# Cosine attention and MLP mixer: early token weights, w2 placed in slot 1, k squares on GpSimd, a moved cast of v, three output tiles

## The chip, the cores and the metric

The kernel runs on one core of one Trainium2 chip. The metric is the device time of one execution in microseconds (us), as the median of several executions. The profile is one execution; its span, from first to last instruction, is 1.7 to 1.9 us shorter than the device time of the same execution.

## The reference

```python
def _attn_ref(q, k, v, tau):                  # q, k, v: (8, 12, 448, 64) float32, tau = 0.1
    q_n = q / (np.linalg.norm(q, axis=-1, keepdims=True) + 1e-06)
    k_n = k / (np.linalg.norm(k, axis=-1, keepdims=True) + 1e-06)
    scores = np.matmul(q_n, k_n.transpose(0, 1, 3, 2)) / tau
    ...                                       # softmax over the last axis
    return np.matmul(attn, v)

def _moe_ref(x, w_tok1, w_tok2, w_ch1, w_ch2):  # x: (8, 448, 768), heads side by side
    xt = x.transpose(0, 2, 1)
    h = np.maximum(xt @ w_tok1, 0.0) @ w_tok2     # 448 -> 256 -> 448, along the tokens
    u = x + h.transpose(0, 2, 1)
    h2 = np.maximum(u @ w_ch1, 0.0) @ w_ch2       # 768 -> 1536 -> 768, along the channels
    return u + h2
```

## The kernel before

The kernel works on pairs of heads; there are 48. Its main loop has slots: slot i computes the scores and exponentials of pair i, and beside them attention times v of the pair before, the token mixing of pairs still earlier, the normalisation of pairs to come, and pieces of the channel mixing of finished batches. A pair's q and k are squared and summed, turned into reciprocal norms on ScalarE, scaled on GpSimd (`kq`), transposed on TensorE (`pst`) and copied by VectorE (`qk`); only then can TensorE start its scores (`psS`). The parts concerned:

```python
outp = ctx.enter_context(tc.tile_pool(name="outp", bufs=2))      # output tiles ost
...
def weights_tok():                     # token weights, float32 in memory, cast by the DMA
    nc.gpsimd.dma_start(out=w1t[:, 0:NC, :], in_=moe_w_tok1[0:SM].rearrange(...))
    nc.gpsimd.dma_start(out=w1t[0:XR, NC, :], in_=moe_w_tok1[SM:S])
    w2n.append(mix.tile([P, TT, S], FP16, name="w2n", tag="gt16", bufs=1))
    nc.gpsimd.dma_start(out=w2n[0][:], in_=moe_w_tok2.rearrange(...))

def place_w2():                        # w2 in the token order of the other tiles
    nc.vector.tensor_copy(out=w2t[:, :, XR:S]..., in_=w2n[0][:, :, 0:SM]...)   # "main copy", 768 columns
    nc.vector.tensor_copy(out=w2t[:, :, S:S + XR], in_=w2n[0][:, :, SM:S])     # 128 columns

def place_w2_odd():
    nc.vector.tensor_copy(out=w2t[:, :, 0:XR], in_=w2n[0][:, :, SM:S])         # "last copy", 128 columns

def cast_v(n):                         # half n of v (six heads), float32 to float16
    (nc.vector if n < 3 else nc.gpsimd).tensor_copy(out=vts[n % NV]..., in_=vm[n]...)
...                                    # before the loop:
        squares_x(0, nc.scalar, nc.gpsimd)
        rnorms(0, 21, 33)
        scaled(1, nc.gpsimd)
...
        score_x(0)
        weights_tok()
        cast_vx(0)
        cast_v(0)
        scaled(2, nc.gpsimd)
        for i in range(NP_ALL + 2):
...                                    # slot i, first slots:
                score(i, 0, 2 if i < 4 else 0); score(i, 1); score(i, 2)
            for p in sum_at.get(i, ()):
                norm_sums(p)           # VectorE sums of squares
...
            casts()                    # slot 3: cast_v(1)
...
            if i: pv(i - 1)            # attention times v; VectorE: reciprocal, x
...
            if i in (0, 1, 2, 4): next_qk(i + 1)     # VectorE copies q and k of the next pair
...
            if i == 2: place_w2()      # end of slot 2
            if i == 3: place_w2_odd()  # end of slot 3
```

Of the kernel before, what the change touches and what calls it, by code (L numbers as in the profile page):

```python
# [22 lines left out]
def kernel(  # L23
# [12 lines left out]
    nc = tc.nc  # L36

    B, H, S, E = q.shape
# [5 lines left out]
    NC = 3  # L44
    SM = P * NC
# [22 lines left out]
    mix = ctx.enter_context(tc.tile_pool(name="mix", bufs=2))  # L68
    outp = ctx.enter_context(tc.tile_pool(name="outp", bufs=2))
    ps = ctx.enter_context(tc.tile_pool(name="ps", bufs=2, space=bass.MemoryType.PSUM))  # L70
# [68 lines left out]

    def weights_tok():  # L140
        nc.gpsimd.dma_start(out=w1t[:, 0:NC, :], in_=moe_w_tok1[0:SM].rearrange("(p c) t -> p c t", c=NC))
        nc.gpsimd.dma_start(out=w1t[0:XR, NC, :], in_=moe_w_tok1[SM:S])
        w2n.append(mix.tile([P, TT, S], FP16, name="w2n", tag="gt16", bufs=1))
        nc.gpsimd.dma_start(out=w2n[0][:], in_=moe_w_tok2.rearrange("(tt p) s -> p tt s", p=P))

    def place_w2():
        nc.vector.tensor_copy(out=w2t[:, :, XR:S].rearrange("t a (c p) -> t a c p", c=NC),
                              in_=w2n[0][:, :, 0:SM].rearrange("t a (p c) -> t a c p", c=NC))
        nc.vector.tensor_copy(out=w2t[:, :, S:S + XR], in_=w2n[0][:, :, SM:S])  # L149

    def place_w2_odd():
        nc.vector.tensor_copy(out=w2t[:, :, 0:XR], in_=w2n[0][:, :, SM:S])

# [33 lines left out]
    def squares_x(n, eq, ek):  # L187
        square(eq, sqx[0:XR, 0:6], xh(xq, n, 6))
        square(ek, sqx[:, 6:9], xh(xk, n, HP))
# [257 lines left out]
    def at(slots):  # L447
        got = {}
        for p, s in slots.items():
            got.setdefault(s, []).append(p)  # L450
        return got


    FIRST = NPAIR
    early_sq = {3: 0, 4: 1, 5: 1, 6: 3, 7: 4, 8: 5, 9: 5, 10: 6, 11: 7, 12: 8, 13: 9, 14: 9, 15: 10, 16: 11, 17: 11}
    sq_slot = {p: early_sq.get(p, p - 6) for p in range(3, NP_ALL)}
    sq_at = at(sq_slot)
    sum_at = at({p: s + 1 for p, s in sq_slot.items() if p < 8 or p >= 18})

    rn_at = {}  # L460
    for n in range(1, NHALF):
        for c0, c1 in ((0, 21), (21, 45)) if n < 4 else ((0, 45),):
            s = 1 + sq_slot[3 * n + (0 if c1 == 21 else 2)]
            rn_at.setdefault(s, []).append((n, c0, c1))
# [7 lines left out]
    xv_at = at({b: {1: 1, 2: 9}.get(b, 6 * b - 4) for b in range(1, B)})  # L472
    cast_at = at({n: {1: 3, 2: 6}.get(n, 3 * n - 2) for n in range(1, NHALF)})
    castx_at = at({n: {1: 2, 2: 6}.get(n, 3 * n - 2) for n in range(1, NHALF)})
# [37 lines left out]
    with tc.manual_schedule():  # L512
# [54 lines left out]
        tpose_main(0, pst, 1)  # L567
        squares_x(0, nc.scalar, nc.gpsimd)
        rnorms(0, 21, 33)
        scaled(1, nc.gpsimd)  # L570
# [17 lines left out]
        score_x(0)  # L588
        weights_tok()
        cast_vx(0)  # L590
        cast_v(0)
        scaled(2, nc.gpsimd)
        for i in range(NP_ALL + 2):
# [30 lines left out]
            def next_sq(ps):  # L624
                for p in ps:
                    norm_begin(p, nc.scalar if p < 18 else nc.gpsimd, nc.scalar if p == 3 else nc.vector if p in (10, 11, 12, 15) else nc.gpsimd)

# [20 lines left out]
            for p in sum_at.get(i, ()):  # L648
                norm_sums(p)
            if i < FIRST:  # L650
                norm_rn()
# [78 lines left out]
            if i == 2:  # L730
                place_w2()
            if i == 3:
                place_w2_odd()
        for p in ut_at.get(NP_ALL + 2, ()):
# [37 lines left out]
```

## Time and profile before

| | before |
|---|---|
| device time, median of the first three runs | 394.86 us (394.48 to 395.2) |
| span of the profile | 392.9 us |
| TensorE busy | 378.7 us, 96% |
| TensorE waiting for w2's copies, once | 1.14 us, at 27.5 us |
| TensorE waiting for an output tile, once | 1.13 us, at 94.8 us |
| VectorE without a hole | 30.7 to 35.0 us |

The lines behind this table stand in the prediction. In a timeline line the first number is the start in us from the beginning of the span, the second the length, then engine, source line, operation, output and input tiles with their shapes and the number of instructions merged into the line; the bracket at the end is the idle time just before it and what ended it. Starts also show more than lengths: the next instruction of an engine can start a little before the recorded end of the one before (in the prediction's lines VectorE's copy of 25.62 ends at 25.62 + 1.09 = 26.71, and the next starts at 26.63), so a cost on an engine's path is best read from start to start.

Four more lines of the kernel before carry the argument, two on VectorE, one on GpSimd, one on TensorE:

```profile
31.07 0.48 DVE L152 COPY w2t<-w2n 128x128 f16<-128x128 f16 x1
31.47 0.94 DVE L193 TENSOR_REDUCE ssq<-sq 128x12 f32<-128x768 f32 x1
30.67 0.82 POOL L211 TENSOR_TENSOR kq<-km,rn 128x384 f16<-128x384 f32 x1
51.57 0.35 PE L308 MATMUL psX<-qk 128*128 128x448 f16 x1 [0.51 <-ACT pt L302]
```

The first is w2's last copy, 0.3 us into the stretch of VectorE without a hole; the copy of pair 5's q and k, at 34.35, starts 3.28 us after it. The second is what VectorE does next, sums of squares, and the third is GpSimd's scaling of pair 5's k, which runs while the copy does. The fourth is a matmul of a later slot that waits 0.50 or 0.51 us for ScalarE in every kernel of this study; it serves as a milestone. What comes after it is 392.9 - 51.57 = 341.33 us.

### The profile page before, as it was taken

What the parts mean: (1) busy time and instruction counts of PE and PEld (TensorE: products, weight loads), DVE (VectorE), ACT (ScalarE), POOL (GpSimd) and SP (SyncE); (2) the same over time, 40 slices, a digit from 0 to 9 for tenths busy, and PEclk for the clock granted to TensorE, in tenths of its full rate; (3) what the DMA queues carried; (4) which work ended last, traced back from release to release, by engine and by line L of the source; (5) the groups of instructions that cost most, each with busy time, mean ns of one, the idle gap of its engine ahead of it and who ended that gap; (6) DMA issues with size and microseconds to landing.
All of it is one profiled execution on the core that took longest, in us unless ns stands there. A gap on an engine that the chain in (4) does not pass through costs nothing.

```text
span 392.9 us, 9076 instructions
## 1 busy us (share of the span) xinstructions
PE 378.7 (96%) x3658; PEld 228.5 (58%) x3658; DVE 193.5 (49%) x368; ACT 225.8 (57%) x411; POOL 209.6 (53%) x306
## 2 busy tenths in 40 slices
PE   8678999998999999999999999999999999999996
PEld 3346555665565656566556566566566566565554
DVE  5688758865344554545524645345534342333022
ACT  5998698843774639573676446673775536511400
POOL 4978486789267584868572947659561700000000
PEclk9899999999999999999999999999999999999999
DMA  7999999969968987999989899999982452013013
GB/s 203 276 238 253 246 236 215 227 138 264 209 131 190 202 183 179 222 183 208 205 199 198 175 245 216 166 189 182 242 142 56 123 123 68 16 57 102 5 40 120
DMA packets 137514, 67.51 MB, mean 172 GB/s; under 512 B 93248, under 2 KB 134016, under 8 KB 137472
## 3 DMA queue, kind: packets, MB, share of 16 engines
q1 hardware_dynamic: 133296, 61.36, 71.4%
q0 software_dynamic: 3632, 5.18, 7.4%
q8 instruction: 28, 0.46, 0.5%
q10 hardware_dynamic: 544, 0.39, 0.3%
q14 instruction: 14, 0.11, 0.1%
HBM read 43.38 MB, written 11.01 MB: 138 GB/s over the span
## 4 chain that ended last, share of the span: by engine, by line
PE 86%; ACT 6%; DVE 3%; DMA 2%; SPq 1%; issue 1%; ACTq 0%; DVEq 0%
PE psF L404 28%; PE psG L389 27%; PE psO L320 9%; PE psS L301 7%; PE psR L341 5%; PE psU L361 4%; ACT pt L302 3%; PE psO L322 3%; PE psX L308 2%; DMA out_dram<-ost 1%; DMA km<-in_k_dram 1%; PE psU L366 1%; PE pst L243 1%; ACT sq L178 1%; DVE ost L407 1%
## 5 line engine op out<-in xcount | busy, mean ns | idle before, releaser
L302 ACT ACTIVATE pt<-psS 128x896 f16<-128x896 f32 x141 | 119.0, 921 | 65.8 <-PE psS L301 65.5
L389 PE MATMUL psG<-ut,wc1t 128*128 128x448 f16 x576 | 119.5, 353 | 0.2
L404 PE MATMUL psF<-wc2t,gt 128*128 128x384 f16 (+2 forms) x684 | 117.3, 324 | 1.2 <-DVE ost L407 1.1
L391 ACT ACTIVATE gt<-psG 128x448 f16<-128x448 f32 x96 | 51.1, 557 | 73.2 <-PE psG L389 73.2
L404 PEld LDWEIGHTS <-gt 128*128 128x128 f16 x684 | 64.5, 98 | 48.4 <-issue 8.1
L389 PEld LDWEIGHTS <-wc1t 128*128 128x128 f16 x576 | 53.2, 98 | 52.5 <-issue 8.7
L211 POOL TENSOR_TENSOR kq<-km,rn 128x384 f16<-128x384 f32 x47 | 39.4, 837 | 80.9 <-ACT rn L204 80.7
L407 DVE TENSOR_TENSOR ost<-psF,ur 128x384 f32<-128x384 f32 (+2 forms) x57 | 31.4, 550 | 90.0 <-PE psF L404 86.6
L320 PEld LDWEIGHTS <-pt 128*128 128x128 f16 x1152 | 50.1, 97 | 8.4 <-issue 2.4
L320 PE MATMUL psO<-vt,pt 128*128 128x65 f16 x1152 | 52.4, 193 | 1.2 <-ACT pt L302 0.8
L326 DVE RECIPROCAL rec<-psO 128x8 f32<-128x8 f32 x48 | 9.9, 207 | 80.9 <-PE psO L322 80.9
L193 DVE TENSOR_REDUCE ssq<-sq 128x12 f32<-128x768 f32 (+1 forms) x49 | 45.1, 929 | 5.3 <-ACT sq L178 3.7
L322 PE MATMUL psO<-vx,pt 128*128 128x130 f16 x192 | 41.8, 218 | 0.0
L180 POOL TENSOR_TENSOR sq<-km 128x384 f32<-128x384 f32 x42 | 34.5, 823 | 13.2 <-DMA km<-in_k_dram 13.0
L211 POOL TENSOR_TENSOR kq<-qm,rn 128x384 f16<-128x384 f32 x47 | 39.5, 841 | 0.0
L301 PE MATMUL psS<-qk 64*128 64x448 f16 x282 | 36.1, 357 | 2.0 <-DVE qk L261 0.9
L327 DVE TENSOR_TENSOR x<-psO,rec 128x512 f16<-128x512 f32 x48 | 33.2, 691 | 1.7
L341 PE MATMUL psR<-x,w1t 128*128 128x128 f16 x384 | 29.2, 219 | 0.1
L309 ACT ACTIVATE pt<-psX 128x448 f16<-128x448 f32 x48 | 27.1, 564 | 3.3 <-PE psX L308 2.3
L361 PE MATMUL psU<-w2t,r 128*128 128x448 f16 x96 | 25.9, 353 | 1.5 <-DVE w2t L149 1.1
L180 POOL TENSOR_TENSOR sq<-qm 128x384 f32<-128x384 f32 x30 | 24.7, 822 | 2.4 <-DVE ssq L193 1.6
L341 PEld LDWEIGHTS <-w1t 128*128 128x128 f16 x384 | 23.8, 97 | 2.1 <-issue 0.3
(76 smaller groups left out, 320.8 us busy)
## 6 DMA issues: line engine op xcount, KB each, us to landing
vm<-in_v_dram SPq DMA_DIRECT2D x16, 576.0 KB, 5.0
out_dram<-ost SPq DMA_DIRECT2D x23, 384.0 KB, 3.1
qm<-in_q_dram SPq DMA_DIRECT2D x14, 576.0 KB, 5.1
km<-in_k_dram SPq DMA_DIRECT2D x14, 576.0 KB, 5.6
wc1t<-in_moe_w_ch_dram POOLq DMA_DIRECT2D x2, 1152.0 KB, 13.8
wc2t<-in_moe_w_ch_dram POOLq DMA_DIRECT2D x2, 1152.0 KB, 12.6
out_dram<-ost SPq DMA_DIRECT2D x9, 192.0 KB, 2.7
xq<-in_q_dram SPq DMA_DIRECT2D x7, 192.0 KB, 5.2
```

Of the source, the lines that this page charges most:

```text
L180: eng.tensor_tensor(out=out, in0=src, in1=src, op=ALU.mult)
L193: nc.vector.tensor_reduce(out=ssqs[p // HP % 3][:, lo + 6 * a0:lo + 6 * a1], in_=sq[p][:, a0:a1].rearrange("p a g e -> p (a g) e"), axis=A ...
L211: eng.tensor_tensor(out=kqs[n % 2][:, j, a, 0:NC, :].rearrange("p c (g e) -> p g c e", g=2), in0=src, in1=_bcast_free(rn, E), op=ALU.mult)
L301: nc.tensor.matmul(psS[:, g, 0:S], qk[r, P * c:P * (c + 1)], qk[r, 512:512 + S], start=True, stop=True)
L302: nc.scalar.activation(out=pt[:, 2 * S * c:2 * S * (c + 1)].rearrange("p (g s) -> p g s", g=2), in_=psS[:, :, 0:S], func=AF.Exp, scale=inv ...
L320: nc.tensor.matmul(psO[:, m, E1 * g:E1 * (g + 1)], pt[:, at:at + P], vt[:, 2 * j + g, c, 0:E1], start=(g == 0 and c == 0), stop=False)
L322: nc.tensor.matmul(psO[:, m, 0:2 * E1], pt[:, PX + P * m:PX + P * (m + 1)], vx[:, j, 0:2 * E1], start=False, stop=True)
L341: nc.tensor.matmul(psR[:, tt, :], w1t[:, m, tt * P:(tt + 1) * P], xs[p][:, m, :], start=(m == 0), stop=(m == NC))
L361: nc.tensor.matmul(psU, rs[p][:, tt, :], w2t[:, tt, lo:lo + S], start=(tt == 0), stop=by_dma and tt == TT - 1)
L389: nc.tensor.matmul(psG[:], wc1t[:, dt, ct * P:(ct + 1) * P], ut[:, dt, sp], start=(dt == 0), stop=(dt == DT - 1))
L391: nc.scalar.activation(out=gt[:, ct, sp], in_=psG[:], func=AF.Relu)
L404: nc.tensor.matmul(psF[:, 0:w], gt[:, ct, lo:lo + P], wc2t[:, ct, P * i0:P * i1], start=(ct == 0), stop=(ct == CT - 1))
```

## The change

The intent is to take away the two waits of TensorE. w2's main copy moves into a hole that VectorE has in slot 1, for which w2 must arrive earlier; so the first token weights are fetched ahead of pair 1's scaling, the second (w2) follows next, and two squares of k leave ScalarE. To unload slot 3, the cast of v's half 1 goes behind w2's last copy. A third output tile takes away the wait near 95 us.

```diff
-    outp = ctx.enter_context(tc.tile_pool(name="outp", bufs=2))
+    outp = ctx.enter_context(tc.tile_pool(name="outp", bufs=3))
...                                     (weights_tok split in weights_tok1(x) and weights_tok2(),
...                                      place_w2 in place_w2() and place_w2_x(lo))
-    early_sq = {3: 0, 4: 1, 5: 1, 6: 3, ...}
+    early_sq = {4: 1, 5: 1, 6: 3, ...}
...
-    cast_at = at({n: {1: 3, 2: 6}.get(n, 3 * n - 2) for n in range(1, NHALF)})
+    cast_at = at({n: {2: 6}.get(n, 3 * n - 2) for n in range(2, NHALF)})
...
         squares_x(0, nc.scalar, nc.gpsimd)
+        weights_tok1(0)
         rnorms(0, 21, 33)
         scaled(1, nc.gpsimd)
...
         score_x(0)
-        weights_tok()
+        weights_tok2()
+        weights_tok1(1)
         cast_vx(0)
         cast_v(0)
+        squares_x(1, nc.scalar, nc.gpsimd)
+        squares(3, nc.scalar, nc.gpsimd)
         scaled(2, nc.gpsimd)
...
             for p in sum_at.get(i, ()):
                 norm_sums(p)
+            if i == 1:
+                place_w2()
...
             if i == 2:
-                place_w2()
+                place_w2_x(S)
             if i == 3:
-                place_w2_odd()
+                place_w2_x(0)
+                cast_v(1)
```

More of the change, by code (lines that the diff above doesn't have):

```diff
@@ L138, in mh, with weights_tok1, weights_tok2 @@
         return at[p // HP][:, 2 * (p % HP):2 * (p % HP) + 2]
-    def weights_tok():
-        nc.gpsimd.dma_start(out=w1t[:, 0:NC, :], in_=moe_w_tok1[0:SM].rearrange("(p c) t -> p c t", c=NC))
-        nc.gpsimd.dma_start(out=w1t[0:XR, NC, :], in_=moe_w_tok1[SM:S])
+    def weights_tok1(x):
+        if x:
+            nc.gpsimd.dma_start(out=w1t[0:XR, NC, :], in_=moe_w_tok1[SM:S])
+        else:
+            nc.gpsimd.dma_start(out=w1t[:, 0:NC, :], in_=moe_w_tok1[0:SM].rearrange("(p c) t -> p c t", c=NC))
+    def weights_tok2():
         w2n.append(mix.tile([P, TT, S], FP16, name="w2n", tag="gt16", bufs=1))
@@ L148, in place_w2, with place_w2_x @@
                               in_=w2n[0][:, :, 0:SM].rearrange("t a (p c) -> t a c p", c=NC))
-        nc.vector.tensor_copy(out=w2t[:, :, S:S + XR], in_=w2n[0][:, :, SM:S])
-    def place_w2_odd():
-        nc.vector.tensor_copy(out=w2t[:, :, 0:XR], in_=w2n[0][:, :, SM:S])
+    def place_w2_x(lo):
+        nc.vector.tensor_copy(out=w2t[:, :, lo:lo + XR], in_=w2n[0][:, :, SM:S])
     def weights_ch1(i):
@@ L454 @@
     FIRST = NPAIR
-    early_sq = {3: 0, 4: 1, 5: 1, 6: 3, 7: 4, 8: 5, 9: 5, 10: 6, 11: 7, 12: 8, 13: 9, 14: 9, 15: 10, 16: 11, 17: 11}
-    sq_slot = {p: early_sq.get(p, p - 6) for p in range(3, NP_ALL)}
+    early_sq = {4: 1, 5: 1, 6: 3, 7: 4, 8: 5, 9: 5, 10: 6, 11: 7, 12: 8, 13: 9, 14: 9, 15: 10, 16: 11, 17: 11}
+    sq_slot = {p: early_sq.get(p, p - 6) for p in range(4, NP_ALL)}
     sq_at = at(sq_slot)
-    sum_at = at({p: s + 1 for p, s in sq_slot.items() if p < 8 or p >= 18})
+    sum_at = at({p: s + 1 for p, s in ({3: 0} | sq_slot).items() if p < 8 or p >= 18})
     rn_at = {}
@@ L462 @@
         for c0, c1 in ((0, 21), (21, 45)) if n < 4 else ((0, 45),):
-            s = 1 + sq_slot[3 * n + (0 if c1 == 21 else 2)]
+            s = 1 + ({3: 0} | sq_slot)[3 * n + (0 if c1 == 21 else 2)]
             rn_at.setdefault(s, []).append((n, c0, c1))
@@ L625, in next_sq @@
                 for p in ps:
-                    norm_begin(p, nc.scalar if p < 18 else nc.gpsimd, nc.scalar if p == 3 else nc.vector if p in (10, 11, 12, 15) else nc.gpsimd)
+                    norm_begin(p, nc.scalar if p < 18 else nc.gpsimd, nc.vector if p in (10, 11, 12, 15) else nc.gpsimd)
             if i == FIRST:
```

## The prediction

> **What bounds the kernel now.** I read the page first: its busy shares and its 40 slices. Then the waits of TensorE, then the timelines of each engine over the first 45 us and around 94 us, and last the DMA view in one-microsecond windows.
>
> ```profile
> span 392.9 us, 9076 instructions
> PE 378.7 (96%) x3658; PEld 228.5 (58%) x3658; DVE 193.5 (49%) x368; ACT 225.8 (57%) x411; POOL 209.6 (53%) x306
> PE   8678999998999999999999999999999999999996
> DMA  7999999969968987999989899999982452013013
> ```
>
> TensorE is busy 378.7 of 392.9 us, so 14.2 us of idle is all that any reordering can win without removing work: 3.6% of the span. The windows view places it: about 3.2 us after 350 us (mostly the last stores), 1.4 us before the first matmul, 3.0 us in 5 to 15 us, 4.1 us in 15 to 40 us, 1.1 us in 40 to 60 us, and 1.4 us in 90 to 110 us. From 110 to 350 us there is no idle at all. The change can act on the stretch from 15 to 40 us and the one near 94 us.
>
> The view of who waited for whom (engine, line, awaited, total us, times, longest):
>
> ```profile
> PE psU L361 <- DVE w2t L149: 1.1, 1, 1.1
> PE psF L404 <- DVE ost L407: 1.1, 1, 1.1
> PE psS L301 <- ACT pt L309: 0.8, 2, 0.6
> DVE ost L407 <- DMA out_dram<-ost: 3.4, 1, 3.4
> ```
>
> The first two are the single waits the change aims at: TensorE waiting for VectorE to place w2, and, at 94.8 us, for an output tile that VectorE could not write because an older tile was still being stored (3.4 us on VectorE, of which 1.1 reached TensorE). Start, duration and preceding idle of the instructions that matter, from the timelines (ACT, then DVE, PE and POOL):
>
> ```profile
> 16.71 0.35 ACT L178 ACTIVATE sqx<-xk 128x192 f32<-128x192 f32 x1
> 17.00 2.54 ACT L302 ACTIVATE pt<-psS 128x896 f16<-128x896 f32 x3
> ...
> 17.32 0.74 DVE L197 TENSOR_REDUCE ssq<-sqx 128x9 f32<-128x576 f32 x1
> 19.14 0.21 DVE L326 RECIPROCAL rec<-psO 128x8 f32<-128x8 f32 x1 [1.08 <-PE psO L322]
> 25.62 1.09 DVE L147 COPY w2t<-w2n 128x768 f16<-128x768 f16 x1
> 26.63 0.81 DVE L149 COPY w2t<-w2n 128x128 f16<-128x128 f16 x1
> 27.36 0.93 DVE L166 CAST vt<-vm 128x1152 f16<-128x1152 f32 x1
> 34.35 0.65 DVE L261 COPY qk<-pst 128x960 f16<-128x960 f16 x1
> ...
> 27.50 0.54 PE L361 MATMUL psU<-w2t,r 128*128 128x448 f16 x2 [1.14 <-DVE w2t L149]
> 35.06 1.04 PE L301 MATMUL psS<-qk 64*128 64x448 f16 x6 [0.56 <-DVE qk L261]
> ...
> 9.10 0.83 POOL L211 TENSOR_TENSOR kq<-km,rn 128x384 f16<-128x384 f32 x1 [1.55 <-ACT rn L204]
> 12.90 0.74 POOL L141 DMA_DIRECT2D w1t<-in_moe_w_tok_dram  x1
> 14.54 0.73 POOL L144 DMA_DIRECT2D w2n<-in_moe_w_tok_dram  x1
> ```
>
> See three things. VectorE has a hole of 1.08 us at 18.06 to 19.14, just the size of the 1.09 us copy of w2. GpSimd has a hole of 1.55 us before 9.10, big enough for one DMA issue of 0.74. And from 30.7 to 35.0 us VectorE has no hole (the windows view gives it 4.93 of 5 us in 30 to 35), ending in the copy of pair 5's q and k for which TensorE waits 0.56 us: that stretch is VectorE-bound, not TensorE-bound.
>
> [...] 7.3 us from issue to landing.
>
> ```profile
> w2n<-in_moe_w_tok_dram POOLq DMA_DIRECT2D x1, 224.0 KB, 7.3
> w1t<-in_moe_w_tok_dram POOLq DMA_DIRECT2D x1, 192.0 KB, 6.3
> q0 software_dynamic: 7, 0.01, 5.9%
> ```
>
> The third line is the queue's activity in the window 16 to 17 us: nothing from 12.90 to 16.7, then the first seven packets, so 3.8 us passed from issue to first byte. [...] here 128x384 takes 0.82 us on GpSimd against 0.55 on VectorE, 1.5 times. [...] here the granted clock is 0.50 from 14 to 17 us, after the sparse stretch 11 to 14, and stays 1.00 through the 1.14 us wait at 27.5. The change does not fill 11 to 14, so I expect the same half-clock piece.
>
> **The change part by part.** (The instruction order of the new kernel is known: TensorE's sequence is identical, ScalarE loses two squares, which GpSimd gains, and VectorE's copies move.)
>
> (1) First token weights, issued at about 7.56 us instead of 12.90: 0.74 us into a hole of 1.55. Free on GpSimd. The transfer (by queue 0's packet time about 1.2 us of all 16 engines) lands in 9.4 to 13 us, where 9 to 11 has DMA shares of only 54% and 44%, about 1.0 us of room. Nothing lost in the loads beyond some tenths, and they have slack.
>
> (2) w2's issue moves from 14.54 to 12.90 us. With the measured 6.3 to 7.3 us it lands at 19.2 to 20.2[...].
>
> (3) Two ScalarE squares (k of pair 3, k's rest) go to GpSimd. By start-to-start spacing they cost ScalarE 0.41 + 0.30 = 0.7 us just before pair 1's exponentials at 17.00. But the scores start on TensorE only at 16.40, at half clock, so the first is ready near 16.8: gain 0.2 us, not 0.7. GpSimd does them in 0.51 + 0.82 us from 15.3, having saved 0.74; pair 2's scaling ends near 18.1, before TensorE's transposes at 19.1. No loss.
>
> (4) w2's main copy goes into the hole at 18.06. If w2 has landed, it ends at 19.1 and costs nothing, and slot 2 loses 1.0 us: the first psU starts at about 26.25 instead of 27.50 (0.2 from part 3, then only the 0.81 us copy ahead, 25.44 to 26.2). If w2 lands at 19.2 to 19.5, VectorE stands still for 1.2 to 1.4 us, reciprocal, x and the copy of pair 2 come that much later, exponentials of pair 2 start near 22.2 to 22.4 instead of 21.73 (less, as ScalarE was late anyway), and psU starts at about 26.9 to 27.05: still 0.5 better.
>
> (5) The cast of v half 1 (0.93, spacing 0.9) moves from 27.36 to after slot 3's last w2 copy. That puts 0.9 us into the VectorE-bound stretch. I carried the durations on: in the good case VectorE reaches that cast at 30.2, sums to 32.6, ut, reciprocal and x to 33.9, and the copy for pair 5 begins at 33.9 instead of 34.35: of 1.25 us only 0.45 is left. In the middle case the same chain gives a copy at about 34.6 to 34.75, a loss of 0.2 to 0.4. After 36 us TensorE has enough work queued, so this difference stays to the end.
>
> (6) Third output tile: the 1.13 us wait at 94.8 goes, as nothing older than three tiles is still being stored. It should persist, since TensorE shows no idle from 110 to 350. Cost in SBUF only.
>
> Sum: good case 0.45 + 1.13 = 1.6 us; middle case 1.13 - 0.3 = 0.8 us; and w2 landing at 20.2 costs about 1 us more in VectorE's chain: about 0.
>
> **Rivals.** *A wait for w2's DMA takes the place of the wait for its copy.* For: the 7.3 and 6.3 us to landing and the full DMA from 11 to 21 us (shares 0.9 to 1.2). Against: the larger part of queue 0's own backlog, the first weights, is out of its way. It makes 394.0 to 395, and in a bad run 395.5. *VectorE in slot 4 is the bound, so all that slot 3 gains is given back.* For: no hole from 30.7 to 35.0, and the cast is put right there; this is already in my sum. Full strength, only the output tile's 1.1 us is left: 393.7. *ScalarE is the bound from 13.6 to 25 us (4.95 and 4.89 busy of 5 us), so the squares are worth their whole 0.7 us.* Against: the half-clock scores at 16.4. With it, and w2 in time: 392.8. *An early DMA delays v or pair 4's k:* v half 0 landed at 13.1 us, needed only at 18, so little.
>
> **Range and chances.** I weigh good, middle and late w2 at 0.4, 0.45 and 0.15: 0.64 + 0.36 + 0 = 1.0 us of gain, and add 0.2 for output waits that the new slack may spare: 394.86 - 1.2 = 393.7 us. Eight times in ten between 392.4 (all of ScalarE's 0.7 and a full slot 3) and 395.0 (w2 late, run-to-run spread of 0.7 us between the three runs before). Faster by over 2% would need 7.9 us, more than all the idle these parts touch (4.1 + 1.4): 0.01. Slower by over 2% would need a new stall of 8 us: 0.01. Within 2%: 0.98.
>
> **What would show it.** TensorE's wait for w2t gone or under 0.2 us; no wait of VectorE for the stores near 92 us and no TensorE idle at 94; queue 0 packets near 9.5 to 12 us; pair 1's exponentials at about 16.8. The deciding row is VectorE's w2 copy in slot 1: preceded by an idle ended by w2n's DMA (middle case, 1 us or more) or by none (good). A wait of TensorE in slot 4 for the moved cast, or a longer one than 0.56 us for pair 5's copy, would show part 5. I am wrong if pair 5's scores start before 34.0 (slot 4 is not the bound) or after 36, or if a load of q or k becomes late by the early weights.

The marked cuts are statements that no trace or run of this case shows, among them the good case's time of w2's landing. The sum is 0.64 + 0.36 + 0 + 0.2 = 1.2 us of gain, 394.86 - 1.2 = 393.7 us; but that w2 lands before the hole at 18.06 us, on which the good case's 0.64 rests, was not shown: the 6.3 to 7.3 us measured from issue to landing give 19.2 to 20.2. The 9.4 to 13 us for the first weights are the author's estimate too (in the changed kernel queue 0 moved them from 9.0 to 11.6 us), and the half-clock piece after a sparse stretch is one observation, not a rule (no_early_fetch, below).

## The result, and the profile after

The changed kernel took 394.92 us (median of five, 394.53 to 396.49), the kernel before in the same rounds 394.91 (394.48 to 395.66). The ratio is 1.0005, 95% interval 0.9981 to 1.0028. Here and below a ratio is the mean time of one kernel's fast runs over that of the other's in the same rounds, so not quite the ratio of the medians. The prediction was a gain of 1.2 us; there was none, though the time lies inside the range. All outputs are right.

The head of the page of the changed kernel, and three lines of its view of who waited for whom:

```profile
span 392.9 us, 9074 instructions
PE 377.0 (96%) x3658; PEld 228.3 (58%) x3658; DVE 194.4 (49%) x368; ACT 225.5 (57%) x409; POOL 211.1 (54%) x308
```

```profile
PE psS L304 <- DVE qk L264: 2.8, 2, 1.7
DVE w2t L151 <- DMA w2n<-in_moe_w_tok_dram: 1.1, 1, 1.1
PE psO L323 <- DVE vt L169: 1.1, 1, 1.1
```

Both waits at which the change aimed are gone, for w2's copy and for the output tile, and the span is the same 392.9 us. Three new ones stand in their place: VectorE waits 1.1 us for w2's DMA, TensorE 1.1 us for the moved cast, and TensorE waits twice, 2.8 us together, for copies of q and k. Where they lie, from the timelines of VectorE, TensorE and GpSimd of the changed kernel (its line numbers are three higher than before):

```profile
19.70 0.80 DVE L151 COPY w2t<-w2n 128x768 f16<-128x768 f16 x1 [1.11 <-DMA w2n<-in_moe_w_tok_dram]
30.62 0.85 DVE L155 COPY w2t<-w2n 128x128 f16<-128x128 f16 x1
31.38 1.43 DVE L169 CAST vt<-vm 128x1152 f16<-128x1152 f32 x1
32.74 0.94 DVE L196 TENSOR_REDUCE ssq<-sq 128x12 f32<-128x768 f32 x1
35.62 0.65 DVE L264 COPY qk<-pst 128x960 f16<-128x960 f16 x1
...
21.96 0.74 PE L304 MATMUL psS<-qk 64*128 64x448 f16 x6 [1.72 <-DVE qk L264]
27.04 0.54 PE L364 MATMUL psU<-w2t,r 128*128 128x448 f16 x2
32.87 0.36 PE L323 MATMUL psO<-vt,pt 128*128 128x65 f16 x6 [1.07 <-DVE vt L169]
36.33 0.74 PE L304 MATMUL psS<-qk 64*128 64x448 f16 x6 [1.03 <-DVE qk L264]
52.84 0.35 PE L311 MATMUL psX<-qk 128*128 128x448 f16 x1 [0.51 <-ACT pt L305]
...
30.59 0.82 POOL L214 TENSOR_TENSOR kq<-km,rn 128x384 f16<-128x384 f32 x1
31.38 0.82 POOL L214 TENSOR_TENSOR kq<-qm,rn 128x384 f16<-128x384 f32 x1
32.16 1.34 POOL L183 TENSOR_TENSOR sq<-km 128x384 f32<-128x384 f32 x1
```

Read them against those of before. The first psU starts at 27.04 without a wait, 0.46 us earlier than before. VectorE reaches w2's last copy at 30.62, 0.45 earlier. Then the copy for pair 5 comes at 35.62, 1.27 **later** than before: from last copy to that copy it is 5.00 us instead of 3.28. The same 1.27 stands at pair 5's scores (36.33 instead of 35.06) and at the milestone (52.84 instead of 51.57). So 1.72 us were lost between the starts of those two copies, and 0.45 gained before.

The 1.72 can be itemised from start to start. The cast takes 32.74 - 31.38 = 1.36 us of VectorE. The last copy takes 31.38 - 30.62 = 0.76, where before it took 0.40 (31.07 to the sums at 31.47): 0.36 more. Together 1.72.

The 0.36 and the 0.45 belong together. In both kernels the last copy ends 0.06 us after the GpSimd scaling that was running when it began: 31.55 and 31.49 before, 31.47 and 31.41 in the changed kernel (each start plus length). VectorE came to this copy 0.45 us earlier and left it only 0.09 earlier. The loss of 1.27 us at the copy for pair 5 is thus the cast's 1.36 less 0.09.

After the milestone the changed kernel needs 392.9 - 52.84 = 340.06 us, where the kernel before needs 341.33: 1.27 us gained. (Spans are given to 0.1 us, so such a difference from a span is good to 0.05.) This is the output tile, as two runs below confirm. VectorE's write of it, first in the kernel before, then in the changed one:

```profile
94.17 0.56 DVE L407 TENSOR_TENSOR ost<-psF,ur 128x384 f32<-128x384 f32 x1 [3.38 <-DMA out_dram<-ost]
```

```profile
92.70 0.56 DVE L410 TENSOR_TENSOR ost<-psF,ur 128x384 f32<-128x384 f32 x1 [0.65 <-PE psF L407]
```

Before, it waited 3.38 us for an older tile's store; after, 0.65 us for its own matmul. Both executions have the same span because as much was gained after the milestone as was lost ahead of it.

### The profile page after: what moved, and what is told of

The parts are those of the page before. It is cut to its first block, busy times and chain, and to the rows that moved or that the text cites. A ratio compares the mean times of both kernels' runs of the same rounds, so it can differ in the third digit from the quotient of the medians.

```text
span 392.9 us, 9074 instructions
## 1 busy us (share of the span) xinstructions
PE 377.0 (96%) x3658; PEld 228.3 (58%) x3658; DVE 194.4 (49%) x368; ACT 225.5 (57%) x409; POOL 211.1 (54%) x308
## 4 chain that ended last, share of the span: by engine, by line
PE 88%; ACT 5%; DVE 4%; SPq 1%; DMA 1%; issue 1%; DVEq 0%
PE psF L407 28%; PE psG L392 27%; PE psO L323 9%; PE psS L304 7%; PE psR L344 5%; PE psU L364 4%; ACT pt L305 3%; PE psO L325 3%; PE psX L311 2%; PE pst L246 1%; DMA km<-in_k_dram 1%; PE psU L369 1%; ACT sq L181 1%; DVE ssq L196 0%; DVE ut L371 0%
## 5 line engine op out<-in xcount | busy, mean ns | idle before, releaser
L410 DVE TENSOR_TENSOR ost<-psF,ur 128x384 f32<-128x384 f32 (+2 forms) x57 | 31.4, 551 | 87.8 <-PE psF L407 87.8
L183 POOL TENSOR_TENSOR sq<-km 128x384 f32<-128x384 f32 x43 | 35.8, 836 | 8.9 <-DMA km<-in_k_dram 8.7
```

Of the source, the lines that this page charges most:

```text
L183: eng.tensor_tensor(out=out, in0=src, in1=src, op=ALU.mult)
```

## The experiments

Every kernel can be split at the same points: the time t1 at which VectorE starts w2's last copy, the stretch s from there to the copy for pair 5, the way from there to the milestone, and the tail after the milestone. All come from the profiles. The way from pair 5's copy to the milestone can be left out of the argument: it is 17.21 or 17.22 us in thirteen of the sixteen kernels, and 17.38 to 17.42 in the three in which TensorE waited only 0.33 us for that copy (cast_back, odd_late_k6, odd_late). The tails of the fourteen kernels with three tiles agree within what the rounding of the spans allows.

One more thing differs between executions: how long TensorE ran at half clock. In the profiles the granted clock is 0.50 for about 3.4 us where its mean is 0.996 (before from 14.0 to 17.4 us, changed from 14.9 to 18.3, before_3_tiles_hole). Where the mean is 0.990 or 0.991 (the other twelve) it is twice that: 6.8 or 6.9 us in the six whose windows view covers it whole (in one piece in two_tiles, three_tiles_alone, k67_on_scalar, odd_late and changed_again, in two of 3.4 us in no_early_fetch). Where it is 0.987 (v_cast_later) it is about three times that: 6.8 us by the windows view, and a later stretch in which the psX matmul at 25.81 us takes 0.55 us instead of 0.35. One stretch below counts 3.4 us. At 0.50 it takes 1.7 of 392.9 us off the mean, 0.004, so by this estimate the mean clock of every execution counts these stretches without a profile. In three_tiles_alone, early_fetch_alone and before_3_tiles_hole the executions with one stretch are 0.25 to 0.5 us faster on average than those with two (393.40 against 393.68, 393.24 against 393.73, 393.23 against 393.48).

| kernel | t1 | s | milestone | tail | median us | ratio to before (95%) |
|---|---|---|---|---|---|---|
| before | 31.07 | 3.28 | 51.57 | 341.33 | 394.91 | 1 |
| changed | 30.62 | 5.00 | 52.84 | 340.06 | 394.92 | 1.0005 (0.9981-1.0028) |
| two_tiles | 31.43 | 5.00 | 53.64 | 341.06 | 396.92 | 1.0050 (1.0034-1.0065) |
| three_tiles_alone | 31.50 | 3.29 | 52.01 | 340.09 | 393.49 | 0.9962 (0.9950-0.9974) |
| cast_back | 30.68 | 3.12 | 51.22 | 340.08 | 394.03 | 0.9972 (0.9960-0.9985) |
| w2_first | 31.50 | 5.00 | 53.72 | 340.08 | 394.75 | 0.9991 (0.9978-1.0004) |
| k67_on_scalar | 30.85 | 3.85 | 51.91 | 340.09 | 393.83 | 0.9962 (0.9930-0.9995) |
| w2_in_slot_2_hole | 30.65 | 4.98 | 52.85 | 340.05 | 394.31 | 0.9968 (0.9937-0.9999) |
| early_fetch_alone | 30.98 | 3.30 | 51.49 | 340.11 | 393.54 | 0.9949 (0.9916-0.9982) |
| before_3_tiles_hole | 30.61 | 3.65 | 51.47 | 340.03 | 393.37 | 0.9942 (0.9912-0.9972) |
| v_cast_later | 32.17 | 5.01 | 54.40 | 340.10 | 395.02 | 1.0006 (0.9993-1.0019) |
| squares_back | 31.93 | 4.51 | 53.66 | 340.14 | 394.70 | 0.9991 (0.9978-1.0004) |
| odd_late_k6 | - | - | 52.15 | 340.05 | 393.68 | 0.9965 (0.9954-0.9977) |
| odd_late | - | - | 51.71 | 340.09 | 393.43 | 0.9945 (0.9925-0.9964) |
| changed_again | 31.35 | 4.99 | 53.55 | 340.05 | 395.07 | 0.9991 (0.9979-1.0003) |
| no_early_fetch | 31.97 | 4.54 | 53.72 | 340.08 | 396.14 | 1.0017 (1.0002-1.0032) |

The kernel before had medians of 394.92 (first four experiments), 395.18 (next four), 395.08 (next three), 395.6 (odd_late) and 395.47 (last two): the groups ran at different times and partly on different chips, so ratios compare better than medians. The profile of a kernel is one execution among five or six and need not be its typical one (cast_back's is the fastest of its five).

In the quoted expectations, theory A says that the third tile keeps its 1.1 us and the rest of the change loses it again; C blames the moved cast in slot 4, D the wait for w2's DMA; E is that w2's last copy and the cast are long there because each waits for the GpSimd operation that is running; G blames the early cast of v's half 0, which waits for its load.

### two_tiles: the changed kernel with two output tiles again

```diff
-    outp = ctx.enter_context(tc.tile_pool(name="outp", bufs=3))
+    outp = ctx.enter_context(tc.tile_pool(name="outp", bufs=2))
```

> The changed kernel with two output tiles again. Theory A (the changed kernel loses 1.27 us by pair 5's scores, at 36.33 against 35.06 us, and wins about 1.13 us back at 94 us through the third tile): the 1.1 us wait of TensorE for the output tile returns near 96 us, and the time is 1.1 to 1.3 us over the kernel before, near 396.1. Rival B (the third tile's gain never reached the end, and the early loss was made good by later slack): the time stays within 0.3 us of the kernel before, 394.9.

Measured 396.92 us (396.06 to 397.8), slower than before with an interval clear of 1. The wait for the output tile is back on TensorE, and the tail is 341.06 instead of 340.06:

```profile
96.57 2.11 PE L407 MATMUL psF<-wc2t,gt 128*128 128x384 f16 x12 [0.85 <-DVE ost L410]
```

So the rest of the change, without the tile, is a loss. It is 0.8 us more than expected; the milestone of this execution is 0.80 later than the changed kernel's, in t1 and not in s. What moves t1 is taken up below; why it should be late in the typical execution of this kernel is not explained. The half-clock stretches don't explain it: five of its six executions have two, as four of the five of changed_again below.

### three_tiles_alone: the kernel before with three output tiles

```diff
-    outp = ctx.enter_context(tc.tile_pool(name="outp", bufs=2))
+    outp = ctx.enter_context(tc.tile_pool(name="outp", bufs=3))
```

> The kernel before with only the third output tile. Theory A: TensorE's 1.13 us idle at 94.8 us goes, nothing takes its place, the time is 393.7 to 393.8 (ratio about 0.997). Rival B: the gain is lost by a later wait (no gain, 394.9).

Measured 393.49 us (393.32 to 393.86): 1.4 us faster than the kernel before by the medians. The wait at 94 us is gone and the tail is 340.09, as in the changed kernel. One line of the change carries its whole gain; the rest takes it away again.

### cast_back: the changed kernel with the cast of v's half 1 in slot 3, as before

```diff
-    cast_at = at({n: {2: 6}.get(n, 3 * n - 2) for n in range(2, NHALF)})
+    cast_at = at({n: {1: 3, 2: 6}.get(n, 3 * n - 2) for n in range(1, NHALF)})
...
                 place_w2_x(0)
-                cast_v(1)
```

> The changed kernel with the cast of v half 1 back at slot 3, before the copy of ut, where VectorE has a hole of 0.82 us. Theory C (most of the loss in slot 4 is the moved cast and w2's last copy, 1.43 and 0.85 us long there beside GpSimd work): pair 5's scores start at 34.9 to 35.2 instead of 36.33, TensorE's 1.07 us wait for the cast goes, the time is 1.1 to 1.4 us below the changed kernel, near 393.6. Rival D (the loss comes from the 1.11 us wait for w2's transfer in slot 1): pair 5's scores stay within 0.4 us of 36.3, time 394.6 to 394.9.

Measured 394.03 us (393.11 to 394.59), 0.9 under the kernel before of the same rounds, with which the changed kernel was level. The decisive line is w2's last copy on VectorE:

```profile
30.68 0.18 DVE L155 COPY w2t<-w2n 128x128 f16<-128x128 f16 x1
```

It starts at the same place as in the changed kernel (30.62), but lasts 0.18 us instead of 0.85: it falls on the seam between two GpSimd instructions (the second starts at 30.71), where in the changed kernel a GpSimd scaling had started just ahead, at 30.59; and without the cast behind it the copy for pair 5 comes 3.12 us later and not 5.00. The wait for w2's DMA is still there, 1.45 us in this execution. So the moved cast is most of the loss (C): the kernel gains although that wait is still there. It need not be all of it: by medians cast_back is still 0.54 us slower than three_tiles_alone, with overlapping intervals, so a smaller share for the wait (D) is not excluded. This profile is the fastest of five executions; its pair 5's scores, at 34.50, are earlier than theory C's 34.9 to 35.2, while the median gain of 0.9 is less than its 1.1 to 1.4. The cast itself is again 1.43 us long at 26.97, but in that place VectorE otherwise stands waiting for psU (0.82 us at 27.81 in the changed kernel).

### w2_first: w2 fetched early, the first token weights in its place

```diff
         squares_x(0, nc.scalar, nc.gpsimd)
-        weights_tok1(0)
+        weights_tok2()
...
-        weights_tok2()
+        weights_tok1(0)
         weights_tok1(1)
```

> The changed kernel with the two fetches exchanged: w2 is fetched at 7.6 us, both parts of the first weights at 13.0. w2 lands near 11.7 us, the 1.11 us wait of VectorE in slot 1 goes, w2's copy starts at 18.5, pair 2's exponentials at about 21.6 instead of 22.36; the first weights land near 19.2, needed at 25.1. Rival D (the wait for w2 is the loss): pair 5's scores 0.8 us earlier at 35.5, time 0.8 us below the changed kernel, near 394.1. Theory C: that 0.8 is won in slot 2 but slot 4 stays VectorE-bound with the same long copies, so the gain at pair 5's scores is 0.8 at most and 0.3 at least, time 394.1 to 394.6.

Measured 394.75 us (394.05 to 395.57). VectorE has no wait for w2 any more, and the milestone is nevertheless later (53.72). Another load became late instead, that of v's half 0, whose cast stands ahead of pair 1's copy:

```profile
15.87 0.76 DVE L169 CAST vt<-vm 128x1152 f16<-128x1152 f32 x1 [2.33 <-DMA vm<-in_v_dram]
```

Pair 1's scores waited 2.04 us behind it and started at 17.25 (in the profiled execution, the slowest of five). The stretch s is 5.00 again. Neither expectation came true: the wait was turned into a new one, and slot 4 did not change.

### k67_on_scalar: GpSimd unloaded in slot 4

k's squares of pairs 6 and 7 go to ScalarE, so that GpSimd is idle while VectorE copies and casts. The cast stays where the change put it.

```diff
-... nc.vector if p in (10, 11, 12, 15) else nc.gpsimd)
+... nc.scalar if p in (6, 7) else nc.vector if p in (10, 11, 12, 15) else nc.gpsimd)
```

> The changed kernel with the k squares of pairs 6 and 7 (and of k's rest) on ScalarE instead of GpSimd, so that GpSimd's scaling of pair 5 runs at 29.3 to 30.9 us and it then rests while VectorE does w2's last copy and the moved cast. Theory E (the two copies are long because each waits for the GpSimd operation that is running: 1.43 is 0.7 of waiting and 0.75 of copying): the copy falls from 0.85 to 0.2 to 0.4 us, the cast from 1.43 to 0.75 to 1.0, TensorE's 1.07 us wait for the cast to 0.2 to 0.5, pair 5's scores come at 35.3 to 35.7 instead of 36.33, time about 0.8 us below the changed kernel, 394.1. Rival F (the copies are long for another reason, the DMA traffic or their shape): durations unchanged, time 394.9 or, by ScalarE's 1.1 us of extra squares, up to 395.5.

Measured 393.83 us (393.66 to 395.72). The same two instructions of VectorE, and the last one of GpSimd before it rests:

```profile
30.85 0.37 DVE L155 COPY w2t<-w2n 128x128 f16<-128x128 f16 x1
31.14 0.75 DVE L169 CAST vt<-vm 128x1152 f16<-128x1152 f32 x1
30.35 0.82 POOL L214 TENSOR_TENSOR kq<-qm,rn 128x384 f16<-128x384 f32 x1
```

The cast takes 0.67 from start to start instead of 1.36, the copy 0.29 instead of 0.76: 1.16 us less, and s falls from 5.00 to 3.85, by 1.15. Pair 5's scores start at 35.40, within theory E's 35.3 to 35.7. Only work of another engine was moved, nothing of VectorE's own. This shows that GpSimd's work lengthens these two. In the changed kernel the cast and GpSimd's scaling both start at 31.38; the scaling keeps its usual 0.82 us, the cast takes 1.43, which is 0.68 over the 0.75 it takes with GpSimd at rest; and the square that GpSimd starts at 32.16, while the cast still runs, takes 1.34 instead of 0.82. So each of the two engines was the longer one in turn, VectorE by 0.68 us, then GpSimd by 0.52; by what mechanism, no run shows. VectorE's sums of squares keep 0.94 to 0.96 us in all these kernels.

The copy again ends with GpSimd's instruction: 30.35 + 0.82 = 31.17, and 31.22. GpSimd's timeline was read for ten of the fourteen kernels that have this copy in slot 3. In nine of them it ends 0.05 or 0.06 us after the GpSimd instruction that was running when it began (in v_cast_later after the one that began 0.02 us ahead of it), so its length, 0.36 to 0.86 us, is what that instruction still had to run. (The tenth is cast_back, where only 0.06 us was left to run and the copy took 0.18.)

### w2_in_slot_2_hole: the changed kernel, main copy one slot later

```diff
-            if i == 1:
+            if i == 2:
                 place_w2()
```

> The changed kernel with w2's main copy not in slot 1 but in slot 2, after the sums and ahead of the reciprocal, where VectorE has a hole of 0.90 us at 23.6 to 24.5. VectorE no longer waits for w2's transfer (landed 19.6): pair 2's scores start at about 20.6 instead of 21.96, its exponentials at 21.3 instead of 22.36, the first psU at about 26.0 instead of 27.04. Slot 4 keeps its long cast, so pair 5's scores come 1.0 us earlier, 35.3, and the time is 1.0 us below the changed kernel, 393.9. If the loss is only in slot 4 (slot 4 refills whatever is won before), the scores stay at 36.0 to 36.3 and the time at 394.6 to 394.9.

Measured 394.31 us (393.69 to 395.02). The copy is at 23.56, takes 0.56 us, and does not wait for w2. The milestone is 52.85, as in the changed kernel (52.84), and pair 5's scores come at 36.34; the median lies between the two expected times. In this execution v's half 0 came 1.85 us late for VectorE, which put pair 1's scores at 16.83 instead of 15.96; and s is 4.98. So this pair of traces shows no gain from taking away the wait for w2: t1 is 30.65 instead of 30.62. But it is not a clean pair, as this execution had two half-clock stretches and the changed kernel's one. By medians this kernel is 0.87 us under the kernel before of its rounds, where the changed kernel was level with it and changed_again 0.40 under. So the wait for w2 may have cost some tenths of a microsecond besides the cast; no run on equal terms settles it.

### early_fetch_alone: the kernel before with three tiles and the first token weights fetched early

```diff
         squares_x(0, nc.scalar, nc.gpsimd)
+        weights_tok1a()          # the main part of w1, out of weights_tok()
         rnorms(0, 21, 33)
```

> The kernel before with three output tiles and one more edit: the first weights are fetched at about 7.6 us as well as at 12.9 (the second fetch writes the same bytes, so the transfer is doubled, but the early one is as in the changed kernel). Theory G (the early fetch pushes back v half 0, whose cast stands before pair 1's copy in VectorE's order; the runs with early fetches showed waits of 0, 1.3, 0 and 2.3 us for it): VectorE waits for v by 0 to 1.5 us, pair 1's scores start 0 to 0.6 us later, time 0.2 to 0.6 us over the 393.5 of three tiles alone. Rival (the fetch fills the idle DMA time at 9 to 11 us and costs nothing): 393.5 within 0.2.

Other than the expectation says, the transfer is not doubled: the edit takes the main part out of `weights_tok()`, and the trace has one fetch of it, at 7.47 us.

Measured 393.54 us (393.23 to 393.95), the same as three tiles alone. VectorE waits 0.73 us for v here, and it does not reach pair 1's scores. The early fetch by itself shows neither a cost nor a gain. That it makes v's half 0 late is likely all the same: VectorE waited 0.73 to 2.33 us for it in seven of the ten profiled kernels with an early fetch, and in none of the five without one whose VectorE timeline was read there.

### before_3_tiles_hole: the kernel before with three tiles and the main copy in slot 2's hole

```diff
+            if i == 2:
+                place_w2()               # after the sums, where VectorE has a hole
...
             if i == 2:
-                place_w2()
-            if i == 3:
-                place_w2_odd()
+                place_w2_x(S)
+            if i == 3:
+                place_w2_x(0)
```

> The kernel before (its fetches, squares and cast as they were) with three output tiles, and only w2's main copy moved from the end of slot 2 into slot 2's hole ahead of the reciprocal (0.97 us of idle at 22.9 to 23.9; w2 landed at 21.8). Theory: nothing waits for w2 there, slot 2's end is 1.0 us shorter, TensorE's 1.14 us wait for w2's copy falls to 0.2 or less, the VectorE chain to pair 5's copy starts 1.0 us earlier, pair 5's scores at about 34.0 instead of 35.06, time 392.4 to 392.8, below both kernels. Rival (the gain is given back in slot 4, as in the changed kernel): 393.5, as with three tiles alone.

Measured 393.37 us (393.14 to 393.53). The wait of TensorE for w2's copy is gone, and psU starts at 26.45, 1.05 earlier than before. By the milestone 0.10 us of it is left (51.47 against 51.57, both with a single half-clock window). A line of TensorE shows where it goes first:

```profile
27.77 0.34 PE L242 MATMUL pst<-id,kq 128*128 128x128 f16 x3 [0.41 <-POOL kq L210]
```

TensorE now waits for GpSimd's scaling, which took 1.45 us there beside VectorE's cast; and w2's last copy takes 0.84 us instead of 0.48 (s 3.65 instead of 3.28). Here the order of the casts is untouched. So removing the wait for w2's copy is worth 0.1 us at the milestone, and the expected 392.4 to 392.8 did not come: slots 3 and 4 take back what was gained.

The traces show how. GpSimd's scaling of pair 5's k ends at 31.39 (31.49 in the kernel before), and the last copy ends with it, at 31.45 (31.55): VectorE came 0.46 us earlier and left 0.10 earlier, which is the 0.10 at the milestone. In the four kernels that leave the cast and all GpSimd instructions of slots 2 to 4 as in the kernel before and this copy in slot 3 (before, three_tiles_alone, early_fetch_alone and this one) the milestone comes 20.02 or 20.03 us after that copy's end. So at this place VectorE's stretch started on GpSimd's schedule, though VectorE arrived 0.46 us earlier. This is read from traces; no run moves GpSimd's work alone in the kernel before.

### v_cast_later: the changed kernel, cast of v's half 0 behind pair 1's copy

```diff
         cast_vx(0)
-        cast_v(0)
...
                 if i in (0, 1, 2, 4):
                     next_qk(i + 1)
+                if i == 0:
+                    cast_v(0)
```

> The changed kernel with the cast of v half 0 moved behind pair 1's q and k copy in VectorE's order. Theory G (in the changed kernel v half 0 lands late in most executions, because the early weights share the DMA, and its cast holds up pair 1's copy: profiled waits of 1.3, 1.6 and 1.9 us in three of five kernels with this start): VectorE's wait for v, if any, comes after pair 1's copy, pair 1's scores start at 15.6 to 16.4 whatever v does, the time is 0.3 to 0.7 us below the changed kernel, 394.2 to 394.6, with less spread. Rival (waiting for w2's transfer until 19.7 hides all that happens to pair 1): 394.9.

Measured 395.02 us (394.77 to 396.25). Pair 1's scores start at 16.34 with no wait for v, so the edit did what it was meant to do; but w2's main copy was only at 19.96 and took 1.22 us beside GpSimd, t1 came to 32.17 and s is 5.01. (The profile is the slowest of six executions and has a third half-clock stretch, between 22.6 and 26.2 us by the lengths of its matmuls, so its t1 is not typical.) Theory G, that the late v is what costs the time, found no support: without it the median, 395.02, is no better.

### squares_back: the changed kernel, both k squares on ScalarE again

```diff
-        squares_x(1, nc.scalar, nc.gpsimd)
-        squares(3, nc.scalar, nc.gpsimd)
+        squares(3, nc.scalar, nc.scalar)
+        squares_x(1, nc.scalar, nc.scalar)
```

> The changed kernel with the k squares of pair 3 and of k's rest back on ScalarE. Theory: part 3 of the change is worth nothing here, since pair 2's scores wait for VectorE's wait for w2 (to 19.7 us): pair 1's exponentials start 0.2 to 0.6 us later, pair 2's within 0.2 us of 22.4, time within 0.3 us of the changed kernel's 394.9. Rival (GpSimd's extra 1.3 us of squares delays sums and scaling, so that undoing it helps): 394.3 or less; (ScalarE was the bound): 395.5.

Measured 394.7 us (394.53 to 395.54), not different from the changed kernel. Pair 1's exponentials start at 17.00 instead of 16.56, and pair 2's at 22.40 against 22.36: w2's arrival decides there, and the wait for it is simply 1.97 us instead of 1.11. Part 3 of the change is worth nothing in this kernel. (This profile, the slowest of five, has its second half-clock stretch late, between 24.0 and 27.6 us by the lengths of its matmuls (psX at 24.57 takes 0.58 us instead of 0.35), and psU at 28.35; its t1 of 31.93 goes with that.)

### odd_late_k6 and odd_late: can the slot-2 hole be turned into time?

Both start from before_3_tiles_hole and put w2's last copy out of slot 4, to the end of slot 5; odd_late_k6 also gives k's squares of pair 6 to ScalarE.

```diff
-            if i == 3:
+            if i == 5:
                 place_w2_x(0)
...                                   (odd_late_k6 only:)
-... nc.scalar if p == 3 else ...
+... nc.scalar if p in (3, 6) else ...
```

> A candidate to beat both kernels: the kernel before with three output tiles, w2's main copy in slot 2's hole, w2's last copy (needed only by the second batch) moved out of slot 4's stretch to slot 5's end, and the k squares of pair 6 on ScalarE. Theory (pair 5's copy is bound by VectorE's chain from 30 to 34 us, where the last copy took 0.84 us beside GpSimd): the chain is 0.76 us shorter than in the run with the hole alone, pair 5's scores at 34.2 to 34.4 instead of 34.96, time 392.6 to 392.9 against 393.4 for it and 393.5 for three tiles alone. Rival (ScalarE is the next bound, its exponentials of pair 5 cannot start before 35.3): 393.2 to 393.5.

Measured 393.68 us (393.1 to 393.99), milestone 52.15; pair 5's scores at 35.43 and not at 34.2 to 34.4. ScalarE has no hole from 31.73 us on and takes 0.2 us (17.42 instead of 17.22 on the way to the milestone). The rest lies ahead: this execution had two half-clock stretches, that of before_3_tiles_hole one, and pair 2's scores came at 22.05 instead of 20.73.

> As the run with the last copy late and pair 6's squares on ScalarE, but with those squares left on GpSimd. There ScalarE had no hole from 24 to 38 us (its squares took 0.7 us ahead of pair 3's rest, and pair 4's scores waited for VectorE's x[...]). Theory H (the squares on ScalarE ate the gain of the late copy): pair 3's rest 0.7 us earlier, pair 5's scores at 34.2 to 34.4 where one half-clock window is seen (34.6 to 34.8 with two), time 392.9 to 393.1. Rival (ScalarE is full there anyway, so nothing on VectorE pays): 393.3 to 393.6, as the other kernels with three tiles.

Measured 393.43 us (392.82 to 394.15), milestone 51.71, which is 0.3 earlier than three_tiles_alone's 52.01 and far from a microsecond; pair 5's scores at 35.04, where 34.6 to 34.8 were expected with two half-clock stretches. So theory H was not borne out. The two ran in different groups, so whether odd_late is better at all is not settled.

### changed_again: the changed kernel once more

The only edit is a comment. It was run because the milestones of the changed front (52.84, and 53.64 in two_tiles) differ more than the executions of one kernel were expected to.

> The changed kernel itself (only a comment added), as the partner of the next run on one chip, and as a second draw of its first 50 us. If the first 50 us cost 1.3 us as in its first profile: 394.8 to 395.0 (ratio 1.000), TensorE's first matmul after ScalarE's wait, near 52 us in all traces, at 52.8. If the run with two tiles showed the usual case (late v, two half-clock windows): that matmul at 53.4 to 53.7, time 395.5 to 395.9 (ratio 1.001 to 1.003).

Measured 395.07 us (394.44 to 395.41), milestone 53.55, t1 31.35, s 4.99. So t1 is a draw: the changed front gave 30.62, 31.43 and 31.35, the front of before 31.07 and 31.50. In this execution both loads were late, v by 1.01 us and w2 by 0.93 us of VectorE's time, and TensorE ran at half clock for 6.8 us, from 15.6 to 22.4, instead of 3.4. The stretch s is not such a draw: 5.00, 5.00 and 4.99 against 3.28 and 3.29. (It is 4.51 and 4.54 in squares_back and no_early_fetch, where the last copy took only 0.36 and 0.38 us; in squares_back it met a GpSimd instruction 0.30 us before its end.)

### no_early_fetch: the changed kernel, no early fetch, w2 ahead of the first weights

```diff
         squares_x(0, nc.scalar, nc.gpsimd)
-        weights_tok1(0)
...
         weights_tok2()
+        weights_tok1(0)
         weights_tok1(1)
```

> The changed kernel without the early fetch: at 13.0 us GpSimd issues w2 first, then both parts of the first weights. v half 0 lands before 14 us and VectorE does not wait for it; GpSimd does not wait for v's rest; w2 still lands near 19.3 to 19.7, so VectorE waits 1 to 1.5 us for it as before. If the early fetch costs something in this kernel: 0.3 to 0.6 us below the run beside it. If only the wait for w2 and slot 4's long copies matter (theory C and E): within 0.2 us of it.

Measured 396.14 us (394.91 to 396.73), about 1 us slower than changed_again beside it. v was in time, w2's DMA was waited for 1.34 us, and pair 2's scores came at 22.07 after 1.86 us of idle on TensorE. What follows is seen in the view of two-microsecond windows (length, then each engine's busy time, the granted clock, the DMA share and GB/s):

```profile
20.00:22.00 2.00, 0.21 (x1) 0.00 (x0) 1.94 (x5) 1.66 (x5) 1.67 (x3) 1.00 1.19 296
...
24.00:26.00 2.00, 2.00 (x25) 1.71 (x22) 0.85 (x2) 1.90 (x7) 0.00 (x0) 0.50 1.19 230
```

TensorE is busy 0.21 of 2.00 us in 20 to 22, and in 24 to 26 its clock is 0.50; psU starts at 28.39 instead of 27.04 (28.35 in squares_back, which has such a late stretch too). The changed kernel had its 0.50 windows near 15 to 18 and was at 1.00 here, with nearly the same sparse stretch (0.28 of 2.00 us). Ahead of the 0.50 in no_early_fetch TensorE had idled 1.86 us in one piece and was busy 1.30 of 2.00 us in 22 to 24 (1.37 in the changed kernel). So of two sparse stretches nearly alike one was followed by half clock and the other was not; executions show one, two, or a later half-clock stretch, and what decides it is not shown, as no run controls it. Nor is it shown that this explains the slower median. The profiled execution, 395.59, is only 0.18 above that of changed_again (395.41), and the one execution with a single half-clock stretch took 395.99; why four of the six take 395.99 or more no trace shows. The early fetch, at any rate, is not what costs the change its time.

## Why the prediction was wrong

**Part 6, the third tile: right.** 1.13 us were predicted to go and to stay gone. The tail is 341.06 to 341.33 us in the two kernels with two tiles and 340.03 to 340.14 in the fourteen with three: 1.0 to 1.3 us.

**Parts 2 and 4, w2's arrival: the middle case came.** w2's copy started at 19.70 after a wait, pair 2's exponentials at 22.36 (22.2 to 22.4 foreseen), psU at 27.04 (26.9 to 27.05 foreseen). The fetch took 6.6 us to land where 6.3 to 7.3 were taken; the earlier landing that the good case needs did not come, as queue 0 moved nothing from 13.03, when w2 was issued, to 17.1 us (in the kernel before, 3.8 us passed from the first issue to the first byte). The first weights, issued at 7.60, ahead of two microseconds in which the kernel before had DMA shares of 0.54 and 0.44, landed in 4.1 us instead of 6.3. The prediction gave the better case a weight of 0.4 all the same, which is 0.2 us of its 1.2.

**Part 3, the squares: right** in that they were not worth their 0.7 us; instead of the 0.2 allowed they brought nothing that the time shows (squares_back).

**Part 5, the cast in slot 4: this step failed, in its size.** The mechanism was named, a VectorE-bound stretch into which the cast is put, and the sign that the prediction gave for it came: TensorE waited 1.07 us for the moved cast and 1.03 instead of 0.56 for pair 5's copy. The cost was taken over from the slot it came from: "That puts 0.9 us into the VectorE-bound stretch." The runs show 1.72 us more than before from the last copy to pair 5's copy: the cast 1.36, because it starts together with a GpSimd instruction, and w2's last copy 0.36, because it ends 0.06 us after GpSimd's scaling in both kernels, though it starts 0.45 us earlier. The prediction's middle case puts the copy for pair 5 at 34.6 to 34.75; it came at 35.62, 0.9 to 1.0 us later. So two terms were wrong: the cast's cost, and that what is gained ahead of the last copy carries on behind it. k67_on_scalar shows that GpSimd's work makes the greater part of the 1.72: s falls by 1.15 us when GpSimd is unloaded. The other 0.57 is the cast's own 0.67 us without GpSimd beside it, less the 0.11 by which the copy is shorter there than before (0.29 against 0.40). The prediction did not ask what GpSimd does beside the moved instructions, and carried the durations of one neighbourhood into another.

**The 0.2 us of "output waits that the new slack may spare": did not come.** No tail of a kernel with three tiles is shorter than 340.03.

The sum now: 1.2 predicted = 0.8 (middle case) + 0.2 (weight of the good case) + 0.2 (output waits). Of the middle case, slot 4 took 0.9 more than allowed. That leaves about nothing, as measured. That gain and loss cancel to 0.01 us is chance: t1 alone differs by 0.8 us between executions of the same front. In terms of the split: tail -1.27, s +1.72, t1 -0.45 in the profiled pair.

**The rivals.** "VectorE in slot 4 is the bound, so all that slot 3 gains is given back" was the right one, but the prediction stopped it at "only the output tile's 1.1 us is left": a bound that is made longer gives back more than was gained. A wait for w2's DMA did take the place of the wait for its copy, but cast_back has it too and gains; what it costs beside the cast is not settled. The early DMA does seem to delay v's half 0, for which the prediction saw time until 18 us; but its cast stands ahead of pair 1's copy, at 13.90 us in the changed kernel. That profile shows no wait of VectorE for v, the one of changed_again 1.01 us. The scores of pair 5 started at 36.33: the prediction had said that it would be wrong if they came after 36.

**What stays open.** How much of t1's spread (30.6 to 31.4 in three executions of the changed front) is due to w2's wait, to late v, and to the half-clock windows cannot be told apart with one profile per kernel. By medians the changed kernel trails three_tiles_alone by 1.4 us and cast_back by 0.9; what the other 0.5 is made of is not shown. Why w2's DMA takes 6.6 us was not tried. And two_tiles is slower than its tail accounts for, in the median of its six executions too, though it differs from the changed kernel only near the stores.

A version that beats both kernels is the smallest edit: three output tiles and nothing else (393.49 us, ratio 0.9962). The versions with a further edit of the kernel before are within 0.2 us of it (393.37 to 393.68, in other groups of runs), which does not pay for their complexity.

## What to carry to other kernels

Before an instruction is moved, ask what the *other* engine does at its new place: a VectorE cast that took 0.75 us beside an idle GpSimd took 1.43 beside a busy one, and its duration elsewhere in the trace is no guide. A copy that meets a running GpSimd instruction and ends with it, as w2's last copy does here, may gain little by starting earlier: 0.45 us earlier in was 0.09 earlier out. When a wait goes away and the time does not, split the traces at a point after which everything repeats and compare stretch by stretch; here two stretches and one tail explained 0.00 us as -0.45 + 1.72 - 1.27. And test the simplest part of a change alone first: one changed number carried all of its gain.
